# Adding the low word of the converted weights by an accumulating DMA instead of a VectorE add

## Chip, cores, metric

One core of one Trainium2 chip. The metric is the time in microseconds (us) of the whole program on the device. Each time below is the median of several runs, with their lowest and highest. The clock given with a profile is the mean share of full speed that TensorE's throttle granted it.

## The reference

```python
# attention: batch 4, 8 heads, 768 tokens, head width 48
for t in range(S):
    y[:, :, t] = q_t @ state
    state = state + beta_t * outer(k_t, v_t - state @ k_t)      # k normalized
# feed-forward on the 3072 tokens, 384 -> 1536 -> 384
xn  = x / sqrt(mean(x*x) + 1e-6) * rms_g
out = (silu(xn @ w_gate) * (xn @ w_val)) @ w_out
```

The three weight matrices arrive as float64. The kernel reads them as pairs of 32-bit words and makes float32 of them on the chip, in 18 tiles of 128x768. That conversion is what was changed.

## The kernel before

The attention is computed in blocks on TensorE, with small work on VectorE and ScalarE. The feed-forward of one unit (256 tokens) follows as soon as its attention output y exists. A plan interleaves all this with the conversion: `weights()` is a generator, each `yield` ends one scheduling step, and a tile takes five of them.

```python
def fetch():                                # the next raw tile, 768 KB
    ...
    raw = bits.tile([128, WT], I64, name="raw", bufs=3)
    (nc.sync if i < 3 else nc.scalar if i < 5 else nc.gpsimd).dma_start(out=to, in_=src)

def shrink(raw):                            # the ScalarE step, L225
    top = bits.tile([128, WT], FP32, name="top", bufs=2)
    low, high = words(raw)
    nc.scalar.activation(out=top, in_=high.bitcast(FP32), func=ACTF.Copy, scale=2.0**-112)
    return top

def weights():
    for i, ((dst, src), raw) in enumerate(zip(todo, raws)):
        ...                                 # shift and mask: top -> top
        yield
        ...                                 # or with the sign: top -> top
        yield
        if i + 1 < len(todo):
            tops.append(shrink(raws[i + 1]))
        ...                                 # exponent alone: top -> dst
        yield
        nc.vector.scalar_tensor_tensor(     # low word * 2^-52 * exponent -> dst, L260
            out=dst, in0=low, scalar=2.0**-52, in1=dst, op0=ALU.mult, op1=ALU.mult)
        if i > 1:
            fetch()
        yield
        nc.vector.tensor_tensor(out=dst, in0=dst, in1=top, op=ALU.add)     # L266
        yield
```

`dst` is the place of the tile in the resident weights: `wg_sb` (gate), `wv_sb` (value), `wo_sb` (out). ScalarE does the shrinks in program order among its other work: y, y times rs (rs is one over y's root mean square, from GpSimd), Silu, and the copies of keys and scores.

Of the kernel before, what the change touches and what calls it, by code (L numbers as in the profile page):

```python
# [14 lines left out]
ALU = mybir.AluOpType  # L15
# [12 lines left out]
def kernel(  # L28
# [21 lines left out]
    nc = tc.nc  # L50
# [155 lines left out]
    def fetch():  # L206
        i = len(raws)
        if i < len(todo):
            raw = bits.tile([128, WT], I64, name="raw", bufs=3)
            src = todo[i][1]  # L210
            to = raw if len(src.shape) == 2 else raw.rearrange("p (n m) -> p n m", m=DM)
            (nc.sync if i < 3 else nc.scalar if i < 5 else nc.gpsimd).dma_start(out=to, in_=src)
            raws.append(raw)

    def words(raw):
        two = raw.bitcast(U32).rearrange("p (n two) -> p n two", two=2)
        return two[:, :, 0], two[:, :, 1]

    def shrink(raw):
# [7 lines that stand above are left out]
# [3 lines left out]
# [3 lines that stand above are left out]
            top = tops[i]  # L233
            top_u, dst_u = top.bitcast(U32), dst.bitcast(U32)
            nc.vector.tensor_scalar(
                out=top_u,
                in0=top_u,
                scalar1=3,
                scalar2=0x7FFFFFFF,
                op0=ALU.logical_shift_left,  # L240
                op1=ALU.bitwise_and,
            )
            yield
            nc.vector.scalar_tensor_tensor(
                out=top_u,
                in0=high,
                scalar=0x80000000,
                in1=top_u,
                op0=ALU.bitwise_and,
                op1=ALU.bitwise_or,  # L250
            )
            yield
            if i + 1 < len(todo):
                tops.append(shrink(raws[i + 1]))

            nc.vector.tensor_scalar(
                out=dst_u, in0=top_u, scalar1=0xFF800000, scalar2=None, op0=ALU.bitwise_and
            )
            yield
            nc.vector.scalar_tensor_tensor(  # L260
                out=dst, in0=low, scalar=2.0**-52, in1=dst, op0=ALU.mult, op1=ALU.mult
            )
            if i > 1:
                fetch()
            yield
            nc.vector.tensor_tensor(out=dst, in0=dst, in1=top, op=ALU.add)  # L266
            yield
        bits_pool.close()

    conversion = weights()  # L270

    def convert(steps):
# [664 lines left out]
```

## Time and profile before

| | before |
|---|---|
| time, median (lowest to highest) | 880.5 us (872.4 to 884.4) |
| span of the profiled run, mean granted TensorE clock | 881.2 us, 0.957 |
| waiting time of ScalarE just before the 18 shrinks | 25.6 us |
| software DMA queue (the loads that GpSimd issues) | 13 loads, 3.5% of the 16 engines' time |

The first line of the page gives busy time, its share of the span and the number of instructions of each engine:

```profile
PE 820.0 (93%) x8608; PEld 636.0 (72%) x8608; DVE 410.2 (47%) x1032; ACT 253.6 (29%) x651; POOL 95.3 (11%) x125
```

TensorE (PE) is the bound. The view of one source line, with its idle time in front by what ended it (us, times):

```profile
L225 ACT ACTIVATE top<-raw x18: 879/916/934, 10.7 to 170.1; 128x768 f32<-128x768 f32 x18
...
  DVE wg_sb L266: 16.1, 1
  DMA raw<-in_moe_w_out_dram: 3.4, 1
```

The one wait of 16.1 us is before the shrink at 61.3 us, in the start stage.

### The profile page before, as it was taken

What the parts mean: (1) busy time and instruction counts of PE and PEld (TensorE: products, weight loads), DVE (VectorE), ACT (ScalarE), POOL (GpSimd) and SP (SyncE); (2) the same over time, 40 slices, a digit from 0 to 9 for tenths busy, and PEclk for the clock granted to TensorE, in tenths of its full rate; (3) what the DMA queues carried; (4) which work ended last, traced back from release to release, by engine and by line L of the source; (5) the groups of instructions that cost most, each with busy time, mean ns of one, the idle gap of its engine ahead of it and who ended that gap; (6) DMA issues with size and microseconds to landing.
All of it is one profiled execution on the core that took longest, in us unless ns stands there. A gap on an engine that the chain in (4) does not pass through costs nothing.

```text
span 881.2 us, 20181 instructions
## 1 busy us (share of the span) xinstructions
PE 820.0 (93%) x8608; PEld 636.0 (72%) x8608; DVE 410.2 (47%) x1032; ACT 253.6 (29%) x651; POOL 95.3 (11%) x125
## 2 busy tenths in 40 slices
PE   6428789898999999999999999999999999999998
PEld 5327567676787777787777787777777777777776
DVE  7594758986253491333491333491343491221100
ACT  5503335511434312234212234212234212220101
POOL 3001132300041000131000131000130000000000
PEclk9556889999999999999999999999999999999999
DMA  7722625402231103122103122113121113000000
GB/s 187 184 72 51 181 82 157 130 5 84 48 74 34 42 19 85 38 65 39 37 34 69 38 65 40 36 42 61 38 56 22 37 43 61 2 19 1 19 0 19
DMA packets 147849, 51.05 MB, mean 58 GB/s; under 512 B 140176, under 2 KB 143248, under 8 KB 147760
## 3 DMA queue, kind: packets, MB, share of 16 engines
q1 hardware_dynamic: 123840, 35.34, 17.1%
q0 software_dynamic: 1872, 10.22, 3.5%
q10 hardware_dynamic: 22048, 4.20, 2.4%
q8 instruction: 68, 1.11, 0.5%
q14 instruction: 21, 0.17, 0.1%
HBM read 36.11 MB, written 13.63 MB: 56 GB/s over the span
## 4 chain that ended last, share of the span: by engine, by line
PE 78%; DVE 14%; DMA 2%; issue 2%; SPq 1%; ACT 1%; POOL 1%; ACTq 0%; DVEq 0%; POOLq 0%
PE p_gv L793 38%; PE p_o L780 19%; DVE tmp L443 5%; DVE ttb L452 5%; PE p_g L329 3%; PE p_y L567 2%; PE p_z L623 2%; PE p_k L605 2%; PE p_t L313 2%; PE p_y L605 2%; PE p_v L511 2%; PE p_x L641 2%; PE p_w L518 1%; PE p_z L632 1%; DVE h_f L804 1%
## 5 line engine op out<-in xcount | busy, mean ns | idle before, releaser
L780 PE MATMUL p_o<-wo_sb,h_f 128*128 128x384 f32 x576 | 217.5, 502 | 9.9 <-DVE h_f L804 9.8
L793 PE MATMUL p_gv<-xt,wg_sb 128*128 128x256 f32 x864 | 218.3, 388 | 0.6 <-DVE xt L764 0.6
L793 PE MATMUL p_gv<-xt,wv_sb 128*128 128x256 f32 x864 | 215.8, 386 | 0.0
L793 PEld LDWEIGHTS p_gv<-xt,wg_sb 128*128 128x128 f32 x864 | 161.6, 193 | 40.8 <-issue 1.7
L793 PEld LDWEIGHTS p_gv<-xt,wv_sb 128*128 128x128 f32 x864 | 161.5, 191 | 24.8 <-issue 2.5
L804 DVE TENSOR_TENSOR h_f<-sil,p_gv 128x256 f32<-128x256 f32 x144 | 60.2, 418 | 248.3 <-ACT sil L802 248.1
L802 ACT ACTIVATE sil<-p_gv 128x256 f32<-128x256 f32 x144 | 55.2, 383 | 332.0 <-PE p_gv L793 305.8
L780 PEld LDWEIGHTS p_o<-wo_sb,h_f 128*128 128x128 f32 x576 | 105.2, 192 | 62.8 <-DVE h_f L804 15.1
L443 DVE SCALAR_TENSOR_TENSOR tmp<-gblk,nbeta,ttb 128x31 f32<-128x31 f32 (+15 forms) x186 | 74.7, 402 | 13.9 <-DMA gblk<-gd 8.2
L452 DVE TENSOR_TENSOR ttb<-ttb,tmp 128x31 f32<-128x31 f32 (+15 forms) x186 | 63.6, 342 | 6.4
L343 DVE TENSOR_TENSOR gp<-p_g,mask 64x128 f32<-64x128 f32 (+1 forms) x160 | 37.6, 276 | 35.2 <-ACT gp L339 30.9
L293 POOL TENSOR_TENSOR knrm<-ksum,half 128x8 f32<-128x8 f32 x24 | 40.2, 1679 | 61.0 <-DVE ksum L292 60.9
L749 POOL TENSOR_SCALAR ms<-ms 128x1 f32<-128x1 f32 x24 | 6.5, 273 | 287.3 <-ACT y L741 287.0
L318 ACT COPY kqt<-p_t 128x512 f32<-128x512 f32 x48 | 28.0, 584 | 29.6 <-PE p_t L313 29.0
L548 ACT COPY vs<-p_v 32x256 f32<-32x256 f32 x48 | 17.4, 363 | 53.1 <-PE p_v L511 30.6
L623 PEld LDWEIGHTS p_z<-v_raw,tt 64*64 64x64 f32 x768 | 25.8, 142 | 9.4 <-issue 7.2
L435 POOL MEMSET ttb<- 128x1024 f32 x6 | 5.7, 955 | 240.5 <-DMA td<-ttb 189.1
L329 PE MATMUL p_g<-kqt 64*64 64x192 f32 x640 | 31.2, 330 | 0.0
L641 PE MATMUL p_x<-tt,gp 64*64 64x64 f32 x384 | 29.8, 233 | 0.1
L623 PE MATMUL p_z<-v_raw,tt 64*64 64x48 f32 x768 | 28.8, 227 | 0.0
L511 PEld LDWEIGHTS p_v<-tt,gp 32*32 32x32 f32 x768 | 17.6, 108 | 15.5 <-issue 11.1
L641 PEld LDWEIGHTS p_x<-tt,gp 64*64 64x64 f32 x384 | 26.4, 145 | 2.2 <-issue 1.6
(97 smaller groups left out, 803.7 us busy)
## 6 DMA issues: line engine op xcount, KB each, us to landing
kpad<-in_k_dram SPq DMA_DIRECT2D x24, 192.0 KB, 2.9
qpad<-in_q_dram SPq DMA_DIRECT2D x24, 192.0 KB, 2.7
v_raw<-in_v_dram SPq DMA_DIRECT2D x24, 192.0 KB, 3.0
raw<-in_moe_w_out_dram POOLq DMA_DIRECT2D x6, 768.0 KB, 5.0
out_dram<-o_sb SPq DMA_DIRECT2D x24, 192.0 KB, 1.9
gblk<-gd SPq DMA_DIRECT2D x6, 512.0 KB, 3.3
td<-ttb SPq DMA_DIRECT2D x6, 512.0 KB, 2.6
tt<-td SPq DMA_DIRECT2D x96, 32.0 KB, 2.2
```

The source lines that it names most:

```text
L293: nc.gpsimd.tensor_tensor(out=knrm, in0=ksum, in1=half, op=ALU.pow)
L329: nc.tensor.matmul(to, pair[d, K1 if i else K0], pair[d, places], skip_group_check=True)
L343: nc.vector.tensor_tensor(out=to[p, :, place], in0=p_g[p, :, place], in1=mask[p, i, None].to_broadcast([p.stop, 2, HC]), op=ALU.mult,)
L443: nc.vector.scalar_tensor_tensor(out=tmp, in0=gblk[:, i, None, i + 1 :].to_broadcast(shape), scalar=nbeta[:, c, i : i + 1], in1=ttb[:, 0 : ...
L452: nc.vector.tensor_tensor(out=to, in0=to, in1=tmp, op=ALU.add)
L605: nc.tensor.matmul(p_o[p, 2 * j : 2 * j + 2].rearrange("p h d -> p (h d)"), kq[:, j, place], st[:, j], start=(alone or j == 0), stop=alone ...
L623: nc.tensor.matmul(p_zs[b_z][p, h], tt[b_z][p, h], r[p, h], start=(h == 0), stop=(p is lo), skip_group_check=True,)
L641: nc.tensor.matmul(p_x[lo, h], gp[b_x][hi, h, HC * K0 : HC * (K0 + 1)], tt[b_x][hi, h], skip_group_check=True,)
L780: nc.tensor.matmul(p_o[i], h_f[:, i * C : (i + 1) * C], wo_sb[:, f], start=(f == f0), stop=(f == f1 - 1),)
L793: nc.tensor.matmul(p_gv[:, i], w_sb[:, t, f * 128 : (f + 1) * 128], xt[:, t], start=(t == 0), stop=(t == KT - 1),)
L802: nc.scalar.activation(out=sil, in_=p_gv[:, 0], func=ACTF.Silu)
L804: nc.vector.tensor_tensor(out=h_f, in0=sil, in1=p_gv[:, 1], op=ALU.mult)
```

## The change

The intent was to relieve VectorE of 18 adds of 0.96 us. The low word's share is now computed in `top`, the upper word stands in `dst`, and a DMA adds the one into the other.

```diff
-                out=top_u,
+                out=dst_u,
                 in0=high,                      # or with the sign
...
-                out=dst_u, in0=top_u, scalar1=0xFF800000, scalar2=None, op0=ALU.bitwise_and
+                out=top_u, in0=dst_u, scalar1=0xFF800000, scalar2=None, op0=ALU.bitwise_and
...
-                out=dst, in0=low, scalar=2.0**-52, in1=dst, op0=ALU.mult, op1=ALU.mult
+                out=top, in0=low, scalar=2.0**-52, in1=top, op0=ALU.mult, op1=ALU.mult
             )
             if i > 1:
                 fetch()
-            yield
-            nc.vector.tensor_tensor(out=dst, in0=dst, in1=top, op=ALU.add)
+            nc.gpsimd.dma_start(out=dst, in_=top, accum_op=ALU.add)
             yield
```

One `yield` goes too, so a tile takes four steps of the plan, not five.

## The prediction

> **What bounds the kernel now.** I read the slices of the whole span first, to find where TensorE is not full.
>
> ```profile
> PE   6428789898999999999999999999999999999998
> DVE  7594758986253491333491333491343491221100
> ACT  5503335511434312234212234212234212220101
> PEclk9556889999999999999999999999999999999999
> ```
>
> Each digit is a slice of 22 us. From slice 10 on (220 us) TensorE is full and VectorE mostly is not: nothing done for VectorE there can shorten the run. The weight conversion (18 tiles of 128x768; five VectorE steps and one ScalarE step each) lies wholly in the first 180 us, as the list of the disputed line shows:
>
> ```profile
> L266 DVE TENSOR_TENSOR wg_sb<-wg_sb,top x6: 957/958/960, 17.5 to 142.0; 128x768 f32<-128x768 f32 x6
> L266 DVE TENSOR_TENSOR wv_sb<-wv_sb,top x6: 942/958/959, 71.9 to 162.3; 128x768 f32<-128x768 f32 x6
> L266 DVE TENSOR_TENSOR wo_sb<-wo_sb,top x6: 948/958/959, 96.6 to 179.1; 128x768 f32<-128x768 f32 x6
> ```
>
> So I asked for the busy times of the stages in which it runs beside the matmuls (columns: stretch, length, then busy us and count of PE, PEld, DVE, ACT, POOL; clock; DMA share; GB/s):
>
> ```profile
> 88.00:110.00 22.00, 16.88 (x314) 12.51 (x316) 17.43 (x27) 8.39 (x18) 2.51 (x4) 0.87 0.63 182
> 110.00:132.00 22.00, 19.64 (x254) 15.02 (x253) 12.71 (x23) 8.82 (x19) 7.12 (x9) 0.89 0.28 82
> 132.00:154.00 22.00, 22.00 (x171) 16.65 (x170) 17.69 (x40) 12.11 (x33) 6.19 (x7) 0.93 0.59 153
> 154.00:176.00 22.00, 19.95 (x137) 14.31 (x136) 21.09 (x49) 11.52 (x29) 8.60 (x8) 1.00 0.47 130
> 176.00:198.00 22.00, 19.76 (x76) 15.54 (x77) 18.60 (x46) 2.49 (x6) 0.00 (x0) 0.92 0.02 9
> 198.00:220.00 22.00, 19.27 (x99) 13.60 (x98) 13.61 (x34) 2.26 (x6) 1.11 (x2) 0.92 0.29 84
> ```
>
> TensorE is idle there for 5.1 + 2.4 + 0 + 2.0 + 2.2 + 2.7 = 14.5 us. That is 1.6% of 880 us, and the most a free VectorE could give back in this stage. Only from 154 to 176 us is VectorE the bound (21.1 of 22).
>
> The last view is ScalarE in order of time, just before the first feed-forward matmul:
>
> ```profile
> 85.41 0.49 ACT L741 ACTIVATE y<-p_y 128x384 f32<-128x384 f32 x1 [0.90 <-PE p_y L567]
> ...
> 87.97 0.58 ACT L754 ACTIVATE y<-p_y,rs 128x384 f32<-128x384 f32 x1 [1.14 <-POOL rs L750]
> 88.45 0.92 ACT L225 ACTIVATE top<-raw 128x768 f32<-128x768 f32 x1
> 92.81 0.93 ACT L225 ACTIVATE top<-raw 128x768 f32<-128x768 f32 x1 [3.45 <-DMA raw<-in_moe_w_out_dram]
> 93.64 0.63 ACT L596 COPY state<-p_s 64x192 f32<-64x192 f32 x2
> 94.29 1.28 ACT L802 ACT_TABLE_LOAD   x1
> 95.58 0.39 ACT L802 ACTIVATE sil<-p_gv 128x256 f32<-128x256 f32 x1
> ```
>
> L225 is the conversion's ScalarE step ("shrink"), put into ScalarE's program order among the chain's own work. Here it waited 3.45 us for a load, and the Silu behind it started at 95.58 although its matmuls had been issued by about 91.3. This is what I expect to become common.
>
> **What the Trainium skill says.** (1) "DMA: Bandwidth & Descriptors", SWDGE vs HWDGE vs iDMA: an accumulating DMA can only be issued from GpSimd. The trace has the later raw loads on that same software queue, so the new DMAs stand behind them. (2) Same page, Anatomy of one DMA: about 2.0 us fixed plus bytes/436e3 us. For a raw load (786,432 B) that gives 3.8 us; the trace shows 4.5/5.3/7.6 from issue to landing (minimum, median, maximum), so I use 5. (3) "TensorE: Matmul & The Clock Gate", Architectural detail: ScalarE and VectorE queues are strict FIFO; the rows above agree. (4) Same page, Part 1: after about 3.4 us idle TensorE drops to half clock. The trace agrees: after a 3.8 us TensorE wait ending at 104.9 the granted clock was 0.50 from 106 to 112 us.
>
> **The change part by part.** Removed: 18 VectorE adds of 0.958 us = 17.2 us, of which 14 lie after 70 us. Added: 18 accumulating DMAs of 393,216 B, GpSimd issue about 0.55 to 0.8 us each (as for the raw loads) = some 12 us on an engine busy 11%. The four other VectorE steps keep their sizes. Moved: a tile now has four scheduling steps, not five, so tiles come every 2.4 plan units, not 3.0, and conversion ends 18 steps earlier in the plan.
>
> What matters is a new wait. The helper tile "top" has two buffers. Before, shrink of tile i+2 reused tile i's buffer when VectorE's add was done. Now it waits until tile i's accumulate has landed. The order of the changed program shows three facts: every shrink from tile 2 on waits for the accumulate two tiles back; from tile 2 to 14 GpSimd issues the 768 KB load first and the accumulate after it, on one queue; and the shrinks stay where they were between y, Silu and the copies.
>
> The lag from the end of the low-word step (L260) to the landing: 0.1 wait + 5.0 for the load in front + about 1.7 for the accumulate (estimate: a load's data flow for about 3 us in the slices of 86 to 110 us; half the bytes, plus the target read) = 6.8 us; then 0.92 for the shrink.
>
> Following the order with durations of before, tiles counted from 0, "shift" being the new time less the old:
>
> - Up to 86 us: nearly unchanged. Shrink 2 comes some 3 us late but VectorE was waiting 8.2 us for the block transfer there. Accumulate 3 lands near 70.3, so the copies of p_v end about 72.8, against 72.2 before. Shift 0 to 1.
> - Tile 5's accumulate is issued by GpSimd behind both rs powers (end 87.94) and a load: 87.95 + 5.0 + 1.7 = 94.7. Shrink 7 stands on ScalarE before the second y times rs, which so moves from 87.97 to 95.7. The first p_gv needs both halves. Shift +7.7.
> - Second xt ends 97.4; L260 of tile 6 ends 98.4, of tile 7 (0.55 + 0.96 + 0.56 + 0.96 later) 101.45. The loads and accumulates of both queue: accumulate 7 lands about 109.4, shrink 9 ends 110.3, table load 1.28, first Silu 111.6 against 95.58, first p_o near 112.5 against 98.2. Shift +14.
> - Shrink 10 (about 120) and 11 (about 126) are met by other work: shift stays +14. Shrink 12 stands before y of unit 2: L260 of tile 10 ends 132.5, landing 139.3, shrink 140.2, y there against 121.7: +18.
> - Accumulate 11 is behind ms and rs of that y on GpSimd: issued about 144, lands 149.8, shrink 13 ends 150.7; y times rs and Silu move from 130.5 to 152.8: +22.
> - Shrink 14 ends 160.1 before the last y times rs: +25 on TensorE. Shrink 15 ends 170.7 before the copy of transposed keys at 140.6: +30. Shrink 16 is absorbed. Shrink 17 ends 184.4 before the score copies of 151.2: +33.
>
> After that no shrink remains. VectorE is relieved of nearly five tiles in what was the 152 to 180 us stage, so I give back 5 of the 7.0 us of TensorE idle there. Half-clock stretches after each new gap may cost some 3 us more, but some of these waits will overlap better than my serial reading: I take 3 off for that. Sum: 880.5 + 33 - 5 + 3 - 3 = 908.5; I write 908.
>
> **The rivals.** (A) The accumulate is hidden and VectorE's relief counts: then TensorE fills the holes, at most 14.5 us, likely 5 to 10: 871 to 876. For it: VectorE at 21.1 of 22 us in one stage, and DMA share of only 0.28 to 0.63. Against it: two buffers, and the fixed place of the shrinks. (B) The waits exist but the lag is short, say 4 us, because loads and accumulates overlap on the 16 engines: about seven lags lie in series, so 7 x 2.8 = 20 us less: 889. (C) The accumulating path is slow, say 3 us more each: 7 x 3 = 21 more: 929; TensorE's half clock goes the same way. (D) The traffic (18 x 393 KB read, target read, written) or the port that GpSimd shares with VectorE delays the block transfers at 23 to 31 and 57 to 67 us, which lie on the chain: 2 to 4 us on top of any of these.
>
> **Range and chances.** From (B) to a little beyond (C): 888 to 935. Slower by over 2% means above 898, which needs about half of my shift: 0.76. Within 2%: 0.21. Faster by over 2% would need more than the whole idle time of the stage: 0.03.
>
> **What would show it.** VectorE's 18 adds gone and busy time down about 17 us; L225 on ScalarE with tens of us of idle time before it, ended by the DMA into the weight tiles (before, its waits sum to 25.6 us, mostly one harmless wait of 16.1); second y times rs near 96 and first Silu near 112; TensorE busy unchanged but idle growing by 30 us between 88 and 185, with granted clock near 0.5 to 0.8 there; everything after shifted rigidly. I am wrong if L225 does not wait for these DMAs, if they land within about 3 us of L260, or if the first Silu stays near 96.

## The result

The changed kernel is correct and slower: 922.05 us (919.54 to 923.44, 4 runs) against 880.49 us for the kernel before (872.41 to 884.37, 4 runs). The ratio is 1.048, 95% interval 1.040 to 1.056. Ratios here are the mean time of one kernel's runs over that of the other's runs of the same rounds, so they are not quite the ratios of the medians.

The page of the changed kernel, busy times and then the slices (23.0 us each, as the span is 920.2 us):

```profile
PE 832.7 (90%) x8608; PEld 644.7 (70%) x8608; DVE 394.1 (43%) x1014; ACT 253.3 (28%) x651; POOL 112.7 (12%) x143
...
PE   6437476699899999999999999999999999999998
...
DVE  6764334465815339234358143365143293221110
...
PEclk8557758799999999999999999999999999999999
```

VectorE has lost its 18 instructions and 16.1 us (410.2 to 394.1). GpSimd (POOL) has gained 18 instructions and 17.4 us. The TensorE row (slices counted from 0) now has holes in slices 4 to 7. The loss is made while the conversion runs: from 260 us to 920 us TensorE is busy 653.7 us with 6739 matmuls, and in the kernel before it was busy 654.3 us with 6741 of them from 220 us to 881 us, so what comes after is only shifted. TensorE's busy time itself rose by 12.7 us with the same 8608 matmuls; the mean granted clock was 0.936, against 0.957 before.

The view of the shrink's line, as for before:

```profile
L225 ACT ACTIVATE top<-raw x18: 887/892/933, 10.0 to 195.1; 128x768 f32<-128x768 f32 x18
...
  DMA wo_sb<-top: 24.8, 4
  issue: 22.8, 3
  DMA wv_sb<-top: 21.9, 4
  DMA wg_sb<-top: 20.8, 3
```

The shrinks themselves take as long as before. But ScalarE stands idle before eleven of them, 67.5 us in all, and what ends it is the landing of an accumulating DMA. `wo_sb<-top` in this row is the new DMA. Another 22.8 us, on three more shrinks, are booked as "issue": the trace shows no releaser there. 17.5 of it is on one shrink in the start stage, as the 16.1 us of before were. The line of the new DMA itself, which answers to the list of VectorE's add that the prediction shows:

```profile
L265 POOL DMA_DIRECT2D wo_sb<-top x6: 868/900/1295, 101.0 to 204.9; - x6
...
  ACT top L225: 67.5, 11
DMA to landing us min/median/max: 3.9/6.7/9.9
```

GpSimd takes 0.9 us to issue one. From issue to landing it is 6.7 us in the middle, and ScalarE is the one that waits for it.

ScalarE in order of time, the same stretch as in the prediction (start, duration; in brackets the idle time in front and what ended it):

```profile
88.12 0.58 ACT L753 ACTIVATE y<-p_y,rs 128x384 f32<-128x384 f32 x1 [0.74 <-POOL rs L749]
96.39 0.89 ACT L225 ACTIVATE top<-raw 128x768 f32<-128x768 f32 x1 [7.68 <-DMA wv_sb<-top]
97.17 0.57 ACT L753 ACTIVATE y<-p_y,rs 128x384 f32<-128x384 f32 x1
107.21 0.90 ACT L225 ACTIVATE top<-raw 128x768 f32<-128x768 f32 x1 [9.47 <-DMA wo_sb<-top]
...
114.34 0.89 ACT L225 ACTIVATE top<-raw 128x768 f32<-128x768 f32 x1 [5.70 <-DMA wo_sb<-top]
...
116.55 0.38 ACT L801 ACTIVATE sil<-p_gv 128x256 f32<-128x256 f32 x1
```

The second y times rs had its rs by 89.0, when GpSimd went on to the next load, and starts at 97.17, because a shrink stands in front of it in ScalarE's queue. The first Silu starts at 116.55 after two more such waits; before, it started at 95.58. TensorE needs these y's: it makes their transposes (`p_xt`) for the feed-forward. Its waits for them between 85 and 230 us (total us, times, longest), in the kernel before:

```profile
PE p_xt L763 <- ACT y L754: 3.3, 3, 2.3
```

And in the changed kernel:

```profile
PE p_xt L762 <- ACT y L753: 19.1, 4, 8.0
```

The stretches of the span (length, then busy us and count of PE, PEld, DVE, ACT, POOL; clock; DMA share; GB/s):

```profile
88.00:110.00 22.00, 11.79 (x163) 8.95 (x162) 7.23 (x11) 3.36 (x6) 5.90 (x9) 0.77 0.57 140
110.00:132.00 22.00, 10.22 (x187) 7.11 (x187) 10.02 (x17) 6.80 (x14) 2.87 (x4) 0.65 0.71 161
132.00:154.00 22.00, 18.68 (x212) 13.80 (x212) 10.69 (x19) 4.64 (x10) 7.51 (x8) 0.81 0.35 77
154.00:176.00 22.00, 11.67 (x54) 8.29 (x53) 6.72 (x13) 5.84 (x13) 7.70 (x8) 0.76 0.51 114
176.00:198.00 22.00, 18.55 (x133) 13.51 (x132) 11.91 (x29) 10.79 (x29) 5.32 (x5) 0.84 0.78 172
```

In these five stretches TensorE is busy 70.9 of 110 us, so it idles 39.1 us; before, by the table in the prediction, it was busy 98.2 and idled 11.8. VectorE is nowhere near full: it was relieved, and then waited for the shrinks like the rest (15.1 us, by who waited for L225).

### The profile page after: what moved, and what is told of

It reads as the page before. It is cut to its first block, busy times and chain, and to the rows that moved or that the text cites. A ratio compares the mean times of both kernels' runs of the same rounds, so it can differ in the third digit from the quotient of the medians. Undisturbed runs are those within 1.5% of the kernel's fastest.

```text
span 920.2 us, 20200 instructions
## 1 busy us (share of the span) xinstructions
PE 832.7 (90%) x8608; PEld 644.7 (70%) x8608; DVE 394.1 (43%) x1014; ACT 253.3 (28%) x651; POOL 112.7 (12%) x143
## 4 chain that ended last, share of the span: by engine, by line
PE 69%; DVE 9%; DMA 6%; ACT 2%; issue 1%; POOL 1%; ACTq 0%; SPq 0%; POOLq 0%; DVEq 0%
PE p_gv L792 34%; PE p_o L779 17%; DVE tmp L442 4%; DVE ttb L451 3%; PE p_g L328 3%; DMA wo_sb<-top 2%; PE p_y L566 2%; PE p_k L604 2%; PE p_z L622 2%; PE p_t L312 2%; PE p_y L604 2%; DMA wg_sb<-top 1%; PE p_x L640 1%; PE p_v L510 1%; PE p_w L517 1%
## 5 line engine op out<-in xcount | busy, mean ns | idle before, releaser
L779 PE MATMUL p_o<-wo_sb,h_f 128*128 128x384 f32 x576 | 220.1, 507 | 15.3 <-DVE h_f L803 15.3
L292 POOL TENSOR_TENSOR knrm<-ksum,half 128x8 f32<-128x8 f32 x24 | 43.1, 1797 | 65.3 <-DVE ksum L291 65.3
L225 ACT ACTIVATE top<-raw 128x768 f32<-128x768 f32 x18 | 16.2, 899 | 92.9 <-DMA wo_sb<-top 24.8
L566 PE MATMUL p_y<-u,gp 128*64 128x48 f32 x768 | 28.0, 230 | 3.3 <-DVE u L647 3.3
L328 PEld LDWEIGHTS p_g<-kqt 64*64 64x64 f32 x640 | 23.5, 134 | 10.8 <-issue 5.5
```

The costliest lines, as they stand in the source:

```text
L292: nc.gpsimd.tensor_tensor(out=knrm, in0=ksum, in1=half, op=ALU.pow)
L328: nc.tensor.matmul(to, pair[d, K1 if i else K0], pair[d, places], skip_group_check=True)
L566: nc.tensor.matmul(p_y[p, h], gp[b_y][:, h, HC * place : HC * (place + 1)], u[:, h], start=(c == 0 and h == 0), stop=True, skip_group_chec ...
L779: nc.tensor.matmul(p_o[i], h_f[:, i * C : (i + 1) * C], wo_sb[:, f], start=(f == f0), stop=(f == f1 - 1),)
```

## The experiments

Theory W is the prediction's: the loss is the wait of the shrinks for the landing, through the two `top` buffers. Its rivals here: S, the four-step spacing is what hurts; T, the traffic or the issuing of the new DMAs hurts, whoever waits; D, a special case of T, in which the early accumulates stand in the way of the block transfers (small blocks of scores, written to DRAM and read back in another layout) that the attention needs at 20 to 31 and 57 to 67 us.

The experiments ran in three batches on one chip each. The kernel before ran beside them: 879.94 us (876.81 to 882.66), 879.39 us (877.5 to 884.1) and 878.33 us (874.43 to 885.76). All twelve runs gave correct results.

| kernel | us, median (lowest to highest) | ratio to before, 95% interval |
|---|---|---|
| changed kernel | 922.05 (919.54 to 923.44) | 1.048, 1.040 to 1.056 |
| v1 changed, but VectorE adds | 875.93 (869.2 to 878.55) | 0.994, 0.988 to 1.000 |
| v2 v1 and idle accumulates | 894.37 (888.93 to 897.4) | 1.016, 1.011 to 1.021 |
| v3 changed, more top buffers | 894.65 (886.5 to 896.19) | 1.015, 1.010 to 1.021 |
| v4 changed, accumulate before load | 896.75 (892.61 to 899.27) | 1.019, 1.015 to 1.024 |
| v5 v3, but VectorE adds | 875.26 (870.77 to 883.79) | 0.997, 0.990 to 1.004 |
| v6 v3, DMA for tiles 5 to 17 only | 880.34 (876.21 to 883.4) | 1.002, 0.998 to 1.006 |
| v7 v3, DMA for tiles 0 to 4 only | 881.44 (878.91 to 887.42) | 1.004, 1.000 to 1.009 |
| v8 v2 with 4 KB accumulates | 875.95 (873.48 to 877.77) | 0.997, 0.995 to 0.999 |
| v9 v6 with two top buffers | 917.27 (915.1 to 920.3) | 1.045, 1.039 to 1.050 |
| v10 v9, accumulate before load | 893.31 (892.08 to 896.99) | 1.017, 1.012 to 1.022 |
| v11 changed, five-step spacing | 917.03 (912.79 to 917.69) | 1.042, 1.038 to 1.047 |
| v12 v1 again, five rounds | 873.14 (869.0 to 879.27) | 0.994, 0.990 to 0.999 |

### v1: the changed schedule with the add back on VectorE

```diff
-            nc.gpsimd.dma_start(out=dst, in_=top, accum_op=ALU.add)
+            nc.vector.tensor_tensor(out=dst, in0=dst, in1=top, op=ALU.add)
             yield
```

> The changed kernel with the same four-step schedule, but VectorE does the add again, in the step of the low word; no accumulating DMA. Theory W (ScalarE's shrink waits for the accumulate that last used its top buffer): without the DMA the wait is gone, so 872 to 890 us, and L225 idles under 30 us in all. Rival S (the denser schedule, four steps a tile and not five, packs the conversion so tightly that it blocks the chain): stays above 905 us.

875.93 us, slightly under the kernel before. L225 idled 31.0 us, just over the 30 expected. The denser spacing and the changed roles of `top` and `dst` cost nothing, so rival S falls. All 46 us between v1 and the changed kernel come with the DMA in place of the add. This is also the base for what follows.

### v2: the DMAs without anyone's need for them

To v1, an accumulate of zeros into the finished tile is added. The zeros lie in the place of the last weight tile until that is converted.

```diff
+        nc.vector.memset(todo[17][0], 0.0)
...
             nc.vector.tensor_tensor(out=dst, in0=dst, in1=top, op=ALU.add)
+            if i < 17:
+                nc.gpsimd.dma_start(out=dst, in_=todo[17][0], accum_op=ALU.add)
             yield
```

> As the run before, VectorE adds, and in addition the accumulating DMA of the same size, queue and place is issued for tiles 0 to 16, adding zeros from the region of tile 17 into the finished weight tile. All the traffic, the GpSimd issue and the queueing are there, but no top buffer waits for it. Theory W: within 6 us of the run before (below 896). Rival T (DMA traffic, descriptor writing on GpSimd[...] delay the rest): at least 25 us of the 39 us come back, so above 905.

894.37 us, 18 us above v1. This is a miss for W in its pure form: DMAs on which no shrink waits also cost, though less than half as much as the whole. The first y starts at 90.76, against 80.68 in v1. The matmuls do wait for these landings too, since they read the tile, but only 2.9 us of such waits show (value weights, 85 to 230 us).

### v3: the wait taken away by more buffers

The pool has no room for a third `top` (a build with three failed for want of space). So most tops are placed in weight regions whose own conversion comes later.

```diff
-        top = bits.tile([128, WT], FP32, name="top", bufs=2)
+        i = len(tops)
+        lent = 12 + i % 6 if i < 12 else i + 3
+        top = todo[lent][0] if i < 15 else bits.tile([128, WT], FP32, name="top", bufs=2)
```

> The changed kernel, with the accumulating DMA, but top of tiles 0 to 14 lies in weight regions that are converted only later (six in rotation, then three), so that a shrink reuses a region whose accumulate is six tiles back (tiles 6 to 11) or three (12 to 14). Theory W: 868 to 890 us, L225's idle time falls from 93 us to under 35. Rivals S and T: above 905, since schedule, traffic and queue are those of the changed kernel.

894.65 us, a miss for W by 5 us (868 to 890 expected): 27 of the 42 us between the changed kernel and the kernel before come back, and some 19 us over v1 remain, about as much as in v2. The shrinks idled 39.7 us, not under 35; 8.5 us of it ended with the landing of an accumulate. The first y is late here as well (90.82).

### v4: the accumulate issued before the next load

```diff
+            nc.gpsimd.dma_start(out=dst, in_=top, accum_op=ALU.add)
             if i > 1:
                 fetch()
-            nc.gpsimd.dma_start(out=dst, in_=top, accum_op=ALU.add)
             yield
```

> The changed kernel, two top buffers, but the accumulate is issued before the 768 KB load of the same step and not after it. Theory W with the lag as predicted (load in front): lag from the low-word step to the shrink falls from 7 to 8 us to about 4, over seven to ten waits in series, so 885 to 902 us. If the accumulate itself is the slow part and not the load in front: 910 to 922.

896.75 us, 25 us better than the changed kernel, as expected if the load in front is a large part of the lag. The second y times rs starts at 93.21 (97.17 in the changed kernel), the first Silu at 108.13 (116.55).

### v5: borrowed buffers, VectorE add

```diff
 (v3, and)
-            nc.gpsimd.dma_start(out=dst, in_=top, accum_op=ALU.add)
+            nc.vector.tensor_tensor(out=dst, in0=dst, in1=top, op=ALU.add)
```

> The kernel of v3_more_top_buffers with the add back on VectorE: no accumulating DMA, no short supply of top buffers. It is the base for v3, v6 and v7, which differ from it only in how many tiles are added by DMA. Every theory: within 5 us of v1_vectore_add (875.9). If it is 885 or more, the borrowed buffers themselves cost something, and v3 has to be read against this run and not against v1. If it is below 872, the two buffers were a hidden limit of the kernel before too.

875.26 us: equal to v1 within the intervals. Borrowing costs nothing, and two buffers were no limit as long as VectorE added.

### v6 and v7: DMA for the late tiles only, for the early tiles only

```diff
 (v3, and in v6; v7 has the branches exchanged)
+            if i < 5:
+                nc.vector.tensor_tensor(out=dst, in0=dst, in1=top, op=ALU.add)
+            else:
+                nc.gpsimd.dma_start(out=dst, in_=top, accum_op=ALU.add)
```

> Borrowed buffers; tiles 0 to 4 added by VectorE, tiles 5 to 17 by accumulating DMA. Theory D (the 18 us that remain in v2 and v3 are lost where the early accumulates stand in the way of the block transfers at 20 to 31 and 57 to 67 us): the loss is nearly gone, 875 to 882, first y near 82 us. Theory L (lost later: slower loads, weights that wait for landing, half clock between 88 and 180 us): 888 to 896. If D and L share it, between.

> The complement: tiles 0 to 4 added by accumulating DMA, the other 13 by VectorE, borrowed buffers. Theory D: 888 to 896, with first y near 90 us as in v2 and v3. Theory L: 874 to 881 with first y near 82. The losses of v6 and v7 over v5 should add up to about that of v3 over v5 (some 18 us) if they are separate.

880.34 and 881.44 us. Neither D nor its opposite (L) holds: v6 lies in the range of D, and v7 just above that of L. Each half costs 5 to 6 us over v5 (875.26), and together, in v3, they cost 19, not 11. The four intervals are wide enough to leave some of that gap open.

The profiles do support D in part. In the profiled executions the first y is 10.1 us later in v2 than in v1 (span 11.6 us longer), and, against v5, 10.1 in v3 (span 17.2 longer) and 9.4 in v7 (span 10.3 longer): most of the loss seen there is made before 91 us. But the profiled execution of v7 was its slowest, 887.42 us; the other three took 878.91 to 883.54, so its profile is not typical of its median. In v7, where only the early tiles use the DMA, VectorE waited 11.0 us for the first block transfer, against 2.2 us in v5, and the first y came at 90.05 instead of 80.70. However, the changed kernel itself, with the same early accumulates, waited only 2.2 us there, and its first y came at 85.58. In it, the third shrink is held by the wait, so the raw load that ScalarE issues after that shrink comes at 27.4, when the block transfer is nearly done. In v7 and v3 that load is issued at 23.5 and 22.3, and stands beside the block transfer. That is a reading of the traces and was not tested by a run of its own. v11 speaks against it as the only cause: its load came at 27.8, and the wait was 8.3 us. The kernel before waited 8.2 us there with no accumulate at all.

### v8: the same issues, hardly any bytes

```diff
 (v2, and)
-                nc.gpsimd.dma_start(out=dst, in_=todo[17][0], accum_op=ALU.add)
+                nc.gpsimd.dma_start(out=dst[:, 0:8], in_=todo[17][0][:, 0:8], accum_op=ALU.add)
```

> The kernel of v2_idle_accumulates with each idle accumulate cut to 8 of 768 columns (4 KB in place of 384 KB): the same 17 issues on GpSimd, one hundredth of the traffic. Theory T (the 18 us of v2 are bytes on the 16 DMA engines): within 5 us of v1, 873 to 881. Theory I (issuing on GpSimd[...] or a fixed cost per accumulate): 888 to 896 as in v2.

875.95 us: the loss of v2 is gone. Issuing 17 accumulates on GpSimd costs nothing visible. The 18 us of v2 are the bytes. From issue to landing an accumulate took 7.4 us in the middle in v2 and 4.9 in v8, so the bytes account for 2.5 of it. The software queue's share says how much: 3.5% of 881.2 us before is 30.8 us for 13 loads, or 2.37 us of all 16 engines per load of 786,432 B. In the changed kernel it is 8.2% of 920.2 us, which is 75.5. The difference, 44.6, over 18 accumulates is 2.48 us each. An accumulate of half the bytes thus holds the engines about as long as a full load. (An estimate: the loads are put down as unchanged, and the shares are rounded. With v1 as the base, 3.7% of 875.6 us, a load comes to 2.49 us and an accumulate of v2, 8.1% of 887.2 us, to 2.32.) In v8 the same sums give 0.26 to 0.35 us for each 4 KB accumulate.

### v9: the wait alone

Only the buffers differ between v6 and v9. The accumulates, their tiles and the spacing are the same.

```diff
 (v6, and)
-        top = todo[lent][0] if i < 15 else bits.tile([128, WT], FP32, name="top", bufs=2)
+        top = bits.tile([128, WT], FP32, name="top", bufs=2)
```

> As v6_dma_late_tiles (tiles 0 to 4 added by VectorE, 5 to 17 by accumulating DMA) but with the two top buffers of the changed kernel in place of borrowed ones: it differs from v6 (880.3) only in where the shrinks may write, and from the changed kernel (922) only in that the early block transfers have no accumulate beside them. Theory W (the wait of the shrinks for the landing is the loss): 908 to 918, with the first y near 80 us and the score copies still 40 us or so late. Rival (the loss needs the early accumulates, or the sum of traffic and wait): 885 to 900.

917.27 us against 880.34: the two buffers cost 37 us, most of the whole loss. The longest waits of ScalarE between 88 and 200 us (total us, times, longest), first of v6, where a top in a borrowed place is listed under that place's name:

```profile
ACT wo_sb L227 <- DMA wg_sb<-wo_sb: 6.2, 2, 3.3
ACT top L227 <- DMA wo_sb<-top: 5.9, 1, 5.9
```

And of v9:

```profile
ACT top L225 <- issue: 29.0, 4, 9.2
ACT top L225 <- DMA wv_sb<-top: 12.4, 2, 8.2
ACT top L225 <- DMA wo_sb<-top: 12.4, 2, 9.4
ACT top L225 <- DMA wg_sb<-top: 8.6, 2, 8.3
```

In v6 the shrinks wait 12.1 us for landings. In v9 they wait 33.4 us for landings and 29.0 us more that the profile books without a releaser. These four shrinks start 6.8 to 8.5 us after the issue of the accumulate that frees their buffer, within the range from issue to landing of this run's accumulates (4.4 to 9.0 us), and such waits are absent in v6, so I count them as the same wait. The two profiled spans differ by 39.2 us (913.6 and 874.4). 18.7 us of it is longer TensorE busy time (833.2 and 814.5, same matmuls, mean granted clock 0.938 and 0.965), and the other 20.5 us is idle time.

### v10: the wait, with a shorter lag

```diff
 (v9, with the add, by either way, moved before fetch())
```

> v9 with the accumulate issued before the next raw load, so that it does not stand behind 768 KB on the queue. Theory W with the lag as its size: the lag from low-word step to landing falls by 2 to 3 us, and with it some 8 to 10 waits: 890 to 900. If the position in the queue does not matter: as v9.

893.31 us, 24 us less than v9. The landing of the accumulates, first in v9:

```profile
DMA to landing us min/median/max: 4.4/6.7/9.0
```

In v10:

```profile
DMA to landing us min/median/max: 4.0/4.3/7.4
```

The landing comes 2.4 us earlier in the middle. ScalarE's waits before ten shrinks fall with it, from the 62.4 us of v9 to 44.7 (20.8, 13.0 and 10.9, all ended by accumulates). That is 17.7 us less waiting; the time fell by 24, and the mean granted clock rose from 0.938 to 0.954. So the loss follows the lag, as W says. The number of buffers and the order on the queue are the levers.

### v11: five steps for a tile again

```diff
             nc.gpsimd.dma_start(out=dst, in_=top, accum_op=ALU.add)
             yield
+            yield
```

> The changed kernel with one more scheduling step after the accumulate, so that tiles come as far apart in the plan as before (3.0 units, not 2.4). Theory W: the shrink two tiles on stands one step, some 1.5 us, later in the order, which hides that much of each of some 10 waits: 900 to 914. If the spacing plays no part (VectorE and ScalarE wait in order all the same): 918 to 925.

917.03 us, a miss by 3 us at the upper end: I expected 900 to 914, and the time is nearer to the 918 to 925 of no part for the spacing. The shrinks do wait less and unit 2's y starts at 127.7 rather than 148.6, as W has it. But the conversion now ends later (last shrink at 204.4, not 195.1), and TensorE waits elsewhere, between 85 and 230 us:

```profile
PE p_g L329 <- ACT kqt L318: 12.3, 4, 7.3
PE p_gv L793 <- DMA wv_sb<-top: 6.3, 2, 3.3
```

The matmuls now wait for the weights themselves to land (6.3 us), and the score matmuls wait for ScalarE's copies, which the late shrinks hold up. What was gained early was given back.

### v12: the candidate

> The kernel of v1_vectore_add again with five rounds, as the candidate to beat both kernels: only its four-step spacing (add in the same step as the low-word product) differs from the kernel before. It measured 0.9937 (0.9876 to 0.9999). If that is real: 0.992 to 0.997 with an interval below 1. If it was luck of that chip: 0.998 to 1.003.

The kernel of v1, with five rounds: 873.14 us, ratio 0.994 with an interval of 0.990 to 0.999. The version that beats both kernels is the changed kernel's four-step schedule with the old add on VectorE. It gains half a per cent. No run tells why; it is only shown that it does.

## Why the prediction was right, and where its sizes were off

The time, 922, lies in the range and on its upper side; 908 was 14 us short.

**Removed and added work.** VectorE lost 16.1 us (17.2 predicted). GpSimd gained 17.4, where about 12 was predicted: an issue of an accumulate takes 0.87 to 1.3 us, not 0.53 to 0.8 as the loads did before. (By the prediction's own list 15 of the adds, not 14, lie after 70 us; nothing rests on it.)

**The wait.** Confirmed as the main cause. It is where the prediction put it (L225, ended by the DMA into the weight tiles), and it is worth 37 us by v6 and v9. TensorE met it as the wait for y, 19.1 us against 3.3.

**The lag was the mis-sized term.** The prediction's serial walk held in its order but not in its steps:

| ScalarE work starts at | before | predicted | measured |
|---|---|---|---|
| second y times rs | 88.0 | 95.7 | 97.2 |
| first Silu | 95.6 | 111.6 | 116.6 |
| y of unit 2 | 121.7 | 140.2 | 148.6 |
| y times rs of unit 2 | 130.5 | 152.8 | 160.8 |
| copy of transposed keys | 140.6 | 170.7 | 181.2 |
| score copies | 151.2 | 184.4 | 195.9 |

The shift at the end is 44.7, not 33. The prediction's lag counts 6.7 us from the issue of the load to the landing. Measured from that issue to the start of the shrink released, it was 6.75 to 8.73 us for tiles 5, 6 and 8 to 13, and 10.55 for tile 7, whose load and accumulate queue behind those of tile 6. From the end of L260 of tile 6 to its shrink it was 7.05 us (100.16 to 107.21), and for tile 7 11.1 (103.21 to 114.34), where 7.95 was predicted (101.45 to 109.4). The load in front landed after 5.7 us in the middle instead of 5.0, and the accumulate's bytes took 2.3 to 2.5 by the estimates under v8, not 1.7. Half of a load's data time and a little for the target was too small a measure. This puts Rival C (a slower accumulate) nearer than B. One step failed outright: shrink 10, "met by other work", waited 8.9 us. No run separates what in the 11.7 us of error is lag and what is the lower clock.

The profiled span grew by 39.0, so of the shift of 44.7, 5.7 us were given back later; 5 had been assumed. That this fits is in part luck: the 7.0 us of TensorE idle from which the 5 was taken are those from 154 to 220 us in the prediction's table, and from 152 to 180 us only 4.3 were idle.

**"TensorE busy unchanged"** was wrong. It rose by 12.7 us with the same matmuls, and by 18.7 between v6 and v9. The half-clock term of 3 us was too small for that. The granted clock of 0.65 to 0.84 in the five stretches was foreseen, its price was not. By spans, the 39 us of loss are 12.7 of slower matmuls and 26.3 of idle.

**The rivals.** A (hidden) and B (short lag) did not occur. Rival D, traffic beside the block transfers, was put at 2 to 4 us on top. The changed kernel is 5 us above v9 (922.05 and 917.27), and its first y is as much later (85.58 and 80.31); but the first y of one and the same program also lay 2.4 us apart in two profiles (80.68 in v1, 83.13 in v12), so this agrees only roughly. As a statement about the traffic D was too small: with the wait mostly removed, the bytes still cost some 19 us (v3 over v1), and without need (v2) they cost 18. The wait hides part of that cost (these 19 and the 37 of v9 over v6 are more than the whole 46), and where exactly the 19 us are lost is not fully settled, as v6 and v7 do not add up to it.

By the ratios, one path from v5 to the changed kernel is: late accumulates with buffers to spare, 0.5% (v6); the two buffers, 4.3% (v9); the early accumulates, 0.35%. Another path would split the parts otherwise, because they are not additive.

## What to carry to other kernels

Moving a step to a DMA moved the release of its source buffer from the end of an instruction of 0.96 us to the landing of a transfer, 6.7 us after its issue behind a load on the same queue. Count the buffers against that lag, and look at which in-order engine has to fill the next one and what stands behind it there. If the buffers can't be more, issue the DMA before the large loads (25 us better in v4, 24 in v10); and price an accumulating transfer by a measured one, not by its size: here it held the engines about as long as a load of twice its bytes.

## What the Trainium skill lacked or had wrong

- "DMA: Bandwidth & Descriptors" gives, in its section on the anatomy of one DMA, 2.0 us plus bytes/436e3, which is 2.9 us for the 393,216 B of a tile. It has no cost for an accumulating DMA. Here one took 4.3 us in the middle (4.0 to 7.4) from issue to landing when it was issued ahead of the load (v10), and 6.7 behind it (the changed kernel).
- The same page doesn't say that an accumulate holds the engines longer per byte. By the software queue's share (an estimate) it was 2.3 to 2.5 us, against 2.4 to 2.5 for a plain load of twice the bytes.
- No page gives the time that GpSimd needs to issue an accumulating DMA: 0.87 to 1.3 us in the changed kernel, against 0.53 to 0.8 for plain loads of twice the bytes in the kernel before.
